# S4D layer and gated FFN on Trainium2: the stage-1 order taken from a table of ranks, with first table steps on POOL and norms that may run on DVE

## The chip, the cores and the metric

One core of a Trainium2 chip. The engines that matter are PE (TensorE: matmul; PEld is its weight load), DVE (VectorE), ACT (ScalarE), POOL (GpSimd) and SP (SyncE, which issues the DMAs). Each runs its own instructions in the order in which the program gives them, and waits on semaphores where it needs another engine's result. The metric is device time of one execution, in us; lower is better.

## The reference

One transformer-like layer on a sequence of L = 2048 rows of D = 640 numbers: a modulated LayerNorm, a state-space convolution (S4D, N = 128 states per channel), a residual, a second modulated LayerNorm and a gated FFN of width F = 1728.

```python
mod = (_silu(c) @ w_mod).reshape(c.shape[0], 6, 1, -1)
sa, ca, ga, sb, cb, gb = (mod[:, 0], mod[:, 1], mod[:, 2], mod[:, 3], mod[:, 4], mod[:, 5])
h = _layernorm(x) * (1 + ca) + sa
x = x + ga * A(h)
h = _layernorm(x) * (1 + cb) + sb
x = x + gb * B(h)

def A(u):
    dt = jnp.exp(log_dt)
    A = -jnp.exp(log_A_real) + 1j * A_imag
    C = (C_real + 1j * C_imag) * dt[:, None]
    P = jnp.exp((A * dt[:, None])[:, :, None] * pos[None, None, :])
    K = 2.0 * jnp.einsum("dn,dnl->dl", C, P).real
    y = irfft(rfft(u, 2 * L) * rfft(K, 2 * L), 2 * L)[:L]
    return y + u * D_skip

def B(x):
    return (silu(x @ w1) * (x @ w3)) @ w2
```

## The kernel before

**Stage 1** makes K, the convolution and the residual; **stage 2** is the FFN. Stage 1 works on five blocks of 128 channels. A block has eight chunks of 16 channels, and each half of a block (four chunks) has a table of angles in integers.

- *Tables* (`tables`, tasks `t<block>.<half>.<i>`): `begin` makes five shifted copies of the step (tiles `p`, `step`, from `pS`), `first` a copy of `pB`, and four additions on POOL fill the table.
- *Chunks* (`gen_tasks`, tasks `g<block>.<chunk>.`): `ph` on POOL adds two tables to 1024 angles per partition; `z0` to `z2` on POOL make the sizes (tiles `yy`, `xx`); `s0` to `s4` on ACT are the sines (`tr`, in PSUM); `m0` to `m4` on DVE multiply sizes and sines; `p` on PE sums over the states (`kps`); `r` and `d` copy the result to `ks`.
- *First LayerNorm*: `mean`, `sq` and `hscale` make the statistics (`xs`, `h_st`, `h_mv`, `h_nm`); in `h_tasks`, `l` loads x, `n` (function `h_norm`) normalises into PSUM (`hn`), `x` and `a` on DVE apply the modulation, and `hb` is stored and read again as `xb`.
- *Spectra*: tasks `hh` and `k` are the first transforms of `xb` and `ks` on PE (`ps`), copied to `sp`. Tasks `w<block>.<i>` (`spectrum_tasks`) hold for each of eight groups `f` (`fh`, copied to `hz`), `k` (`fk`), the products `x0`, `x1`, `c` on DVE (`fp`), and for each pair of groups the first inverse transform `z` (`fz`), copied to `zt` (tasks `v0`, `v1`) and stored as `zd`.
- *Ahead of stage 2*: `iz0`, `iz1` read `zd` back, `ir0`, `ir1` (`first_rows`) do the last inverse transform of the first rows (`iy`) on PE with the residual `x` and the LayerNorm statistics `st_n` on DVE; `fw` and `fs` load and split the first FFN weights (`wl`, `w2l`).

The parameters come from `param_tasks`: chain `pa` for all blocks, then `pb` and `pc` for block 0 (k = 0) and for blocks 1 to 4 (k = 1), each step a task, and `turn_steps` (`q<k>.`: transposes `ptp` on PE, copies to `pB`, `pS`, `mag`).

**What sets the order.** Everything of stage 1 is added as a task to a `Plan` (line 101): the engines that it may run on with a duration for each, what it comes after, a rank, and the ring slots that it takes and gives back (for instance two `ph`, two `yy`, two `xx`, three `tr`, four PSUM banks `bank`). `place` (line 119) is a list scheduler with these durations: of the tasks that could start soonest on an engine, the lowest rank goes next, and a task with two engines goes to the one that it would leave first. `run` calls it with ranks that are written by hand; then four times (`ROUNDS`) `back` runs the plan from its end, and `place` takes the late times that result as ranks. The instructions are then written out in that order. On the chip no plan exists: each engine has its order, and semaphores do the rest.

**Stage 2** does the FFN in four blocks of 512 rows, with hidden columns in 14 pieces; its first matmul is `gu` (line 753), and its order doesn't come from the plan.

Of the kernel before, what the change touches and what calls it, by code (L numbers as in the profile page):

```python
# [32 lines left out]
ROUNDS = 4  # L33
# [67 lines left out]
class Plan:  # L101
# [99 lines left out]
    def back(self, rank, order):  # L201

        T = self.tasks
        index = {n: i for i, n in enumerate(T)}
        before, left = {n: list(t[3]) for n, t in T.items()}, dict.fromkeys(T, 0)
        users, taken = {}, {r: [] for r in self.n}
        for n, t in T.items():
            for k in t[7]:
                users.setdefault(k, []).append(n)
        for _, _, _, n in order:  # L210
            for r, x, _ in T[n][6]:
                if len(taken[r]) >= self.n[r]:
                    before[n] += users[r, taken[r][len(taken[r]) - self.n[r]]]
                taken[r].append(x)
        later = {n: [] for n in T}
        for n, x in before.items():
            for a in x:
                later[a].append(n)
                left[a] += 1
        late = {n: len(x) for n, x in later.items()}  # L220
        end, at, free, port, line, table = {}, {}, dict.fromkeys(self.LAG, 0.0), 0.0, 0.0, None
        ready = [n for n in T if not late[n]]
        while ready:
            best = {}
            for n in ready:
                engs, took, _, _, _, shared, _, _, _, dma = T[n]
                c = None
                for j, e in enumerate(engs):
                    s = 0.0
                    for a in later[n]:  # L230
                        s = max(s, end[a] + (self.LAG.get(e, 0.0) if at[a] != e else self.CHAIN.get(e, 0.0)))
                    if e and not dma:
                        s = max(s, free[e])
                    if e and shared and e != "ACT":
                        s = max(s, port)
                    if c is None or s + took[j] < c[0]:
                        c = s + took[j], s, e, j
                best.setdefault(c[2], []).append((c[1], rank[n], index[n], n, c[2], took[c[3]]))
            pick = None
            for c in best.values():  # L240
                m = min(x[0] for x in c) + self.NEAR
                x = min((y for y in c if y[0] <= m), key=lambda y: y[1:3])
                if pick is None or x[:3] < pick[:3]:
                    pick = x
            s, _, _, n, e, took = pick
            ready.remove(n)
            _, _, _, _, _, shared, _, _, tab, dma = T[n]
            if tab and e == "ACT":
                took, table = took + (self.TABLE if table and tab != table else 0.0), tab
            fin = s + took  # L250
            if dma:
                for b in dma:
                    line = max(s, line) + b / self.RATE
                fin = line + self.LAND + self.FLY
            elif e:
                free[e] = fin
                if shared and e != "ACT":
                    port = fin
            end[n], at[n] = fin, e
            for m in before[n]:  # L260
                late[m] -= 1
                if not late[m]:
                    ready.append(m)
        return end
# [12 lines left out]

class K:
# [248 lines left out]
    def tables(self, b, h):  # L527
# [25 lines left out]
        return [(("DVE", "POOL"), (.75, 2.2), begin),  # L553
# [477 lines left out]
    def gen_tasks(self, b):  # L1031
# [33 lines left out]
        for c in range(8):  # L1065
# [7 lines left out]
            for i in range(5):  # L1073
                add(n + f"s{i}", "ACT", 1.02 if i == 2 else .55, lambda c=c, i=i: ch[c][2](i), [n + f"s{i - 1}" if i else n + "ph"], t + 1 + .1 * i,
                    table=None if i == 2 else "sin", take=[] if i == 2 else [("tr", 1)], give=[("ph", n + "ph")] if i == 4 else [])
# [6 lines left out]
            add(n + "r", "ACT", .3, lambda c=c: rows(c), [n + "p"] + ([f"k{b - 1}.{i}.m" for i in range(8)] if b else ["exp0", "q0.t0", "q1.t0"]), t + 3, give=[("kg", n + "p")])  # L1082
            add(n + "d", "DVE", .1, lambda c=c: skip(c), [n + "r"] + (["dsk"] if b == 0 else []), t + 3, give=[("kg", n + "p")])

    def h_tasks(self, b):
        V, A, G = self.nc.vector, self.nc.scalar, self.nc.gpsimd
        add, W = self.plan.add, self.W
        for i in range(4):
# [7 lines left out]
            add(n + "n", "ACT", 1.54, lambda i=i, place=place: self.h_norm(b, i, place()), [n + "l", "hscale"], t, take=[(bank, 1)],  # L1096
# [7 lines left out]
    def first_tasks(self, b, m):  # L1104
# [23 lines left out]
        for i in range(8):  # L1128
# [14 lines left out]
    def spectra_tasks(self, b):  # L1143
# [56 lines left out]
        for i in range(8):  # L1200
# [50 lines left out]
    def param_tasks(self, T, prio):  # L1251
# [35 lines left out]
    def early_tasks(self, e):
# [136 lines left out]
    def weights_of(self):  # L1424
# [38 lines left out]
```

## Time and profile before

| | us |
|---|---|
| median of 3 runs | 1041.65 |
| lowest and highest run | 1037.33, 1042.3 |
| the profiled execution | 1041.82 |
| its span, first to last instruction | 1039.7 |
| PE busy in the span | 896.2 (86%) |
| DVE busy | 657.7 (63%) |
| ACT busy | 522.5 (50%) |
| POOL busy | 271.1 (26%) |
| mean granted clock of PE | 0.947 |

The shares are means over two stages that have little in common: POOL is nearly idle in stage 2, and PE is nearly always busy there. Stage 1 ends at 436.5 us with the first `gu`. A line of the trace gives the start and the duration of an instruction, and in brackets how long its engine had been idle and what ended that. All instructions that a task issues carry the line of the helper that records them (L90 before, L156 with the change), so groups are told apart by tile and shape.

### The profile page before, as it was taken

The page shows a single profiled execution, that of the slowest core. Times are in us where ns is not written, and L with a number is a line of the kernel's source. Part 1 is how long each engine was busy: PE and PEld are TensorE (multiplying, and loading weights), DVE is VectorE, ACT ScalarE, POOL GpSimd, SP SyncE. Part 2 cuts the span into 40 slices and gives each one's busy share as a digit, 9 for nine tenths or more (in the row PEclk, how much of TensorE's full clock was granted, in tenths as well). Part 3 has the DMA queues.
Part 4 walks back from the last instruction along what each step waited for, and adds up shares of the span by engine and source line. Part 5 has one row for each costly group of instructions (what it writes and reads, how often), then busy time and mean ns, then how long its engine had stood idle before and what let it go on. Part 6 is the DMA issues. An engine that isn't in the chain of part 4 may idle for free.

```text
span 1039.7 us, 20267 instructions
## 1 busy us (share of the span) xinstructions
PE 896.2 (86%) x8129; PEld 715.9 (69%) x8129; DVE 657.7 (63%) x1200; ACT 522.5 (50%) x876; POOL 271.1 (26%) x268
## 2 busy tenths in 40 slices
PE   1454676879899986599999999999999999999996
PEld 1123555667688773477788888888888888888884
DVE  6988888898999945467675353464454454544332
ACT  5659798998778851233234252343343333433221
POOL 1785878877888500000000000000000000000000
PEclk9877888999999997599999999999999999999999
DMA  9872443442222393987432354332453333542402
GB/s 197 268 261 59 123 123 85 119 106 63 63 81 46 97 258 114 212 201 169 118 114 77 99 131 113 94 86 74 114 153 88 104 87 89 140 114 76 113 14 51
DMA packets 140998, 122.05 MB, mean 117 GB/s; under 512 B 13416, under 2 KB 124776, under 8 KB 139368
## 3 DMA queue, kind: packets, MB, share of 16 engines
q1 hardware_dynamic: 140904, 120.75, 43.8%
q8 instruction: 64, 1.05, 0.4%
q14 instruction: 30, 0.25, 0.1%
HBM read 99.75 MB, written 20.97 MB: 116 GB/s over the span
## 4 chain that ended last, share of the span: by engine, by line
PE 59%; DVE 1%; DMA 1%; ACT 0%; SPq 0%; issue 0%; ACTq 0%; DVEq 0%
PE gu L753 12%; PE gu L754 12%; PE gu L755 12%; PE acc L788 6%; PE acc L789 6%; PE acc L790 6%; PE iy L647 2%; PE fz L90 1%; PE tp L680 1%; PE to L804 1%; PE fk L90 1%; PE acc L793 0%; PE acc L794 0%; DMA izb<-zd 0%; PE iy L90 0%; PE fh L90 0%
## 5 line engine op out<-in xcount | busy, mean ns | idle before, releaser
L754 PE MATMUL gu<-xl,wh 128*128 128x512 f32 x540 | 212.9, 394 | 0.0
L753 PE MATMUL gu<-xh,wh 128*128 128x512 f32 x540 | 212.5, 394 | 0.5 <-ACT xh L683 0.5
L755 PE MATMUL gu<-xh,wl 128*128 128x512 f32 x540 | 211.9, 392 | 0.0
L658 ACT ACTIVATE wh<-wr 128x640 fp32r<-128x640 f32 x105 | 71.9, 731 | 136.0 <-PE gu L754 134.8
L721 POOL MEMSET w2l<- 64x640 f32 x3 | 1.9, 628 | 451.9 <-PE acc L789 451.9
L753 PEld LDWEIGHTS gu<-xh,wh 128*128 128x128 f32 x540 | 102.1, 189 | 25.6 <-issue 1.0
L754 PEld LDWEIGHTS gu<-xl,wh 128*128 128x128 f32 x540 | 102.0, 189 | 21.9
L755 PEld LDWEIGHTS gu<-xh,wl 128*128 128x128 f32 x540 | 102.0, 189 | 21.9
L788 PE MATMUL acc<-ah,w2h 128*128 128x512 f32 x260 | 103.8, 399 | 0.0
L789 PE MATMUL acc<-ah,w2l 128*128 128x512 f32 x260 | 102.2, 393 | 0.0
L767 ACT ACTIVATE th<-gu 128x512 f32<-128x512 f32 x52 | 31.1, 599 | 136.6 <-PE gu L755 136.6
L768 DVE SCALAR_TENSOR_TENSOR a<-th,gu 128x512 f32<-128x512 f32 x52 | 35.8, 688 | 100.4 <-ACT th L767 100.2
L769 DVE TENSOR_TENSOR a<-a,gu 128x512 f32<-128x512 f32 x52 | 35.8, 688 | 97.0 <-PE gu L755 97.0
L790 PE MATMUL acc<-al,w2h 128*128 128x512 f32 x260 | 96.4, 391 | 0.0
L90 POOL TENSOR_TENSOR yy<-e,e 128x512 f32<-128x512 f32 x80 | 85.0, 1082 | 29.5 <-PE kps L90 25.4
L659 DVE TENSOR_TENSOR wl<-wr,wh 128x640 fp32r<-128x640 f32 x105 | 82.2, 819 | 10.6 <-ACT wh L658 10.6
L90 POOL TENSOR_TENSOR ph<-p,p 128x1024 int32<-128x1024 int32 x40 | 78.3, 1962 | 27.6 <-ACT tr L90 24.6
L90 PE MATMUL kps<-yy,xx 128*32 128x64 f32 x2560 | 53.9, 244 | 33.2 <-DVE xx L90 28.7
L90 PEld LDWEIGHTS kps<-yy,xx 128*32 128x32 f32 x2560 | 47.5, 123 | 47.9 <-issue 40.1
L658 ACT ACTIVATE w2h<-w2r 128x640 fp32r<-128x640 f32 x51 | 37.6, 738 | 81.5 <-issue 42.5
L90 DVE TENSOR_TENSOR yy<-yy,tr 128x512 f32<-128x512 f32 (+1 forms) x80 | 75.6, 945 | 4.6 <-ACT tr L90 4.2
L659 DVE TENSOR_TENSOR w2l<-w2r,w2h 128x640 fp32r<-128x640 f32 x51 | 42.0, 823 | 56.3 <-ACT w2h L658 56.0
(202 smaller groups left out, 1650.5 us busy)
## 6 DMA issues: line engine op xcount, KB each, us to landing
wr<-in_w SPq DMA_DIRECT2D x104, 320.0 KB, 3.9
w2r<-in_w SPq DMA_DIRECT2D x52, 320.0 KB, 3.0
zd<-zt SPq DMA_DIRECT2D x40, 256.0 KB, 2.4
iz<-zd SPq DMA_DIRECT2D x24, 320.0 KB, 6.3
xs<-in_x SPq DMA_DIRECT2D x16, 320.0 KB, 12.2
hs<-hb SPq DMA_DIRECT2D x20, 256.0 KB, 2.5
xb<-hs SPq DMA_DIRECT2D x20, 256.0 KB, 4.8
x<-in_x SPq DMA_DIRECT2D x16, 320.0 KB, 8.7
```

What stands on the lines that cost most here:

```text
L90: self.prev = self.k.order(f(*a, **kw), self.prev)
L658: self.nc.scalar.activation(H, v, AF.Copy)
L659: eng.tensor_tensor(Lo, v, H.bitcast(F32), op=ALU.subtract)
L753: nc.tensor.matmul(pg, wh[:, i, k, :], xh[:, k, :], start=(k == 0), stop=False)
L754: nc.tensor.matmul(pg, wh[:, i, k, :], xl[:, k, :], start=False, stop=False)
L755: nc.tensor.matmul(pg, wl[:, i, k, :], xh[:, k, :], start=False, stop=(k == KT - 1))
L767: nc.scalar.activation(th, gu[0], AF.Tanh, scale=0.5)
L768: nc.vector.scalar_tensor_tensor(a, th, 1.0, gu[0], op0=ALU.add, op1=ALU.mult)
L769: nc.vector.tensor_mul(a, a, gu[1])
L788: nc.tensor.matmul(acc[k], w2h[:, sl], ah, start=(m == 0), stop=False)
L789: nc.tensor.matmul(acc[k], w2l[:, sl], ah, start=False, stop=False)
L790: nc.tensor.matmul(acc[k], w2h[:, sl], al, start=False, stop=(m == 12))
```

## The change

Six things change; what is computed stays the same.

1. A table `RANKS` holds one integer for each task, in the order in which the tasks are added; `place` runs once with it. `back` and the rounds go.
2. `begin` of the first table (block 0, first half) is tied to DVE, the other nine to POOL. Before, the scheduler chose.
3. `h_norm` may run on ACT or on DVE, where it is a `tensor_scalar`. Before, it was tied to ACT.
4. The ten last parameter steps of block 0 (`pc0`) are one task on DVE.
5. Block 1's first statistics move from DVE to ACT (`stat_v`).
6. Some durations that the scheduler reckons with are set to those of a trace, and a table step also waits for `q.v0`.

```diff
-ROUNDS = 4
+RANKS = """
+-1152 -1540 -1534 -1515 -1509 -1417 -1345 -1436 -1412 -1402 -1385 -1330 -1273 -1351 -1452 -1478 -1480 -1475 -1459 -1510 -1507
...
+"""
...
-    def run(self, rounds):
+    def run(self):
 
         T = self.tasks
-        self.order = self.place({n: t[4] for n, t in T.items()})
-        for i in range(rounds):
-            late = self.back({x[3]: -x[1] for x in self.order}, self.order)
-            self.order = self.place({n: -x for n, x in late.items()})
+        found = [int(x) for x in RANKS.split()]
+        assert not found or len(found) == len(T)
+        self.order = self.place(dict(zip(T, found)) if found else {n: t[4] for n, t in T.items()})
...
-        return [(("DVE", "POOL"), (.75, 2.2), begin),
+        return [("DVE", .9, lambda: begin("DVE")) if b == h == 0 else ("POOL", 1.9, lambda: begin("POOL")),
...
-    def h_norm(self, pc, b, out):
+    def h_norm(self, pc, b, out, e):
...
-            self.nc.scalar.activation(out[:, j], x[:, j], AF.Identity, scale=rstd[:, s], bias=nb[:, s])
+            if e == "DVE":
+                self.nc.vector.tensor_scalar(out[:, j], x[:, j], rstd[:, s], nb[:, s], op0=ALU.mult, op1=ALU.add)
+            else:
+                self.nc.scalar.activation(out[:, j], x[:, j], AF.Identity, scale=rstd[:, s], bias=nb[:, s])
...
-                add(n + f"s{i}", "ACT", 1.02 if i == 2 else .55, ...
+                add(n + f"s{i}", "ACT", (.52, .52, .95, .62, .62)[i], ...
...
-            add(n + "n", "ACT", 1.54, lambda i=i, place=place: self.h_norm(b, i, place()), [n + "l", "hscale"], t, take=[(bank, 1)],
+            add(n + "n", ("ACT", "DVE"), (1.95, .85), lambda e, i=i, place=place: self.h_norm(b, i, place(), e), [n + "l", "hscale"], t, take=[(bank, 1)],
...
-            c = chain(f"pc{k}.", end, n, {0: [b]}, prio + .3 + k * later)
+            if k:
+                c = chain(f"pc{k}.", end, n, {0: [b]}, prio + .3 + k * later)
+            else:
+
+                c = "pc0"
+                add(c, "DVE", 3.1, lambda end=end: [f(self.nc.vector) for _, f in end], [b], prio + .3, port=True)
...
-                add(f"stp{b_}", None, 0, None, [q + "v2"])
+                add(f"stp{b_}", None, 0, None, [q + "v0", q + "v2"])
...
-        add("hscale", "DVE", 5.0, scale, ...
+        add("hscale", "DVE", 6.5, scale, ...
...
-            stat=lambda b: 15.0 + 6 * b, stat_v=(1, 3), later=5.0, col=50.0, quick=20.0, late=3.0, tail=S(4))
+            stat=lambda b: 15.0 + 6 * b, stat_v=(3,), later=5.0, col=50.0, quick=20.0, late=3.0, tail=S(4))
```

Durations of `r`, `e`, `h`, `c`, `v` and `fold` in the plan change by a few per cent as well.

How often an instruction stands in the program, before and after: table copies `step<-pS` on DVE 15 and 3, `p<-pS` on DVE 10 and 2, the five POOL operations of `begin` 25 and 45; `hn` on ACT 80 and 28, on DVE 0 and 52; statistics `h_st` on DVE 16 and 8, `xs` sums and `xs` squares on ACT 8 and 12 each; `zt` on DVE 12 and 7, on ACT 28 and 33; sine and exponent table loads on ACT 14 and 12.

The order of the instructions moves at many places. Three of them follow. First DVE at the start, where the last parameter steps of block 0 (tiles `wb`, `xb`, `e11` at 128x128; those at 128x512 belong to blocks 1 to 4) lead to block 0's `pB`. Before:

```order
L90 TENSOR_TENSOR xb_86<-xb_86 128x512
L90 TENSOR_TENSOR e11_120<-e11_120 128x128
L90 TENSOR_TENSOR xb_86<-e21_121 128x512
L90 SCALAR_TENSOR_TENSOR wb_84<-e11_120,wb_84 128x128
L90 SCALAR_TENSOR_TENSOR wb_84<-xb_86,wb_84 128x512
L90 SCALAR_TENSOR_TENSOR xb_86<-e11_120,xb_86 128x128
L90 SCALAR_TENSOR_TENSOR wb_84<-xb_86,wb_84 128x512
L90 SCALAR_TENSOR_TENSOR xb_86<-xb_86,dt_133 128x128
L90 TENSOR_TENSOR e11_120<-e11_120 128x512
L90 TENSOR_SCALAR pB_124<-ptp0_229 128x128
L90 COPY mag_127<-ptp0_229 128x128
```

With the change:

```order
L156 TENSOR_TENSOR xb_86<-e21_121 128x128
L156 SCALAR_TENSOR_TENSOR wb_84<-xb_86,wb_84 128x128 x2
L156 TENSOR_TENSOR e11_120<-e11_120 128x128
L156 SCALAR_TENSOR_TENSOR wb_84<-e11_120,wb_84 128x128
L156 SCALAR_TENSOR_TENSOR xb_86<-e11_120,xb_86 128x128
L156 SCALAR_TENSOR_TENSOR xb_86<-xb_86,dt_133 128x128
L156 TENSOR_SCALAR pB_124<-ptp_243 128x4x128
L156 TENSOR_SCALAR e11_120<-pB_124 128x512
L156 TENSOR_SCALAR pS_125<-pB_124 128x4x128
L156 COPY mag_127<-ptp0_229 128x128
L156 TENSOR_SCALAR pB_124<-ptp0_229 128x128
```

The operations of the other blocks that stood between block 0's steps are behind them now, and the other blocks' `pB`, `e11` and `pS` are in front of block 0's `pB`.

Second, PE from the last product of the last chunk (`kps` with `yy_624`) on, where `ps40i` are first transforms of `xb`, `ps41i` those of `ks` and `fh4i`, `fk4i` the spectra. Before:

```order
L90 MATMUL kps_387<-yy_624_4546,xx_624_4545 32x64 x32
L90 MATMUL ps407_4781<-wk_72,xb_86 64x4x16x2 x8
L90 MATMUL ps410_4814<-wk_72,ks4_4158 64x4x16x2 x8
L90 MATMUL ps411_4829<-wk_72,ks4_4158 64x4x16x2 x8
L90 MATMUL ps412_4839<-wk_72,ks4_4158 64x4x16x2 x8
L90 MATMUL ps413_4849<-wk_72,ks4_4158 64x4x16x2 x8
L90 MATMUL ps414_4865<-wk_72,ks4_4158 64x4x16x2 x8
L90 MATMUL ps415_4875<-wk_72,ks4_4158 64x4x16x2 x8
L90 MATMUL ps416_4885<-wk_72,ks4_4158 64x4x16x2 x8
L90 MATMUL ps417_4895<-wk_72,ks4_4158 64x4x16x2 x8
L90 MATMUL fh40_4905<-sp_85,wb_84 64x128 x8
```

With the change:

```order
L156 MATMUL ps413_4770<-wk_72,ks4_4117 64x4x16x2 x8
L156 MATMUL ps414_4781<-wk_72,ks4_4117 64x4x16x2 x8
L156 MATMUL kps_378<-yy_624_4565,xx_624_4564 32x64 x32
L156 MATMUL ps411_4824<-wk_72,ks4_4117 64x4x16x2 x8
L156 MATMUL ps415_4857<-wk_72,ks4_4117 64x4x16x2 x8
L156 MATMUL ps417_4872<-wk_72,ks4_4117 64x4x16x2 x8
L156 MATMUL ps416_4882<-wk_72,ks4_4117 64x4x16x2 x8
L156 MATMUL fh40_4892<-sp_85,wb_84 64x128 x8
L156 MATMUL fk40_4908<-sp_85,wb_84 64x128 x8
```

Four first transforms stand behind the last product where nine stood. Further on, the two groups of `iy` (of `ir0`) were ahead of the second `fz`, and are ahead of the last pair of spectra now. Before:

```order
L90 MATMUL fh45_5063<-sp_85,wb_84 64x128 x8
L90 MATMUL iy0_0_5079<-iz00_4951,wd_4805 64x512
L90 MATMUL iy0_0_5079<-iz01_4952,wd_4805 64x512
L90 MATMUL iy1_0_5083<-iz00_4951,wd_4805 64x512
L90 MATMUL iy1_0_5083<-iz01_4952,wd_4805 64x512
L90 MATMUL fz410_5099<-fp42_4990,wz_73 128x512
L90 MATMUL fz411_5100<-fp42_4990,wz_73 128x512
L90 MATMUL fz410_5099<-fp42_4990,wz_73 128x512
L90 MATMUL fz411_5100<-fp42_4990,wz_73 128x512
L90 MATMUL fk45_5105<-sp_85,wb_84 64x128 x8
```

With the change:

```order
L156 MATMUL fh45_5033<-sp_85,wb_84 64x128 x8
L156 MATMUL fz410_5044<-fp42_4985,wz_73 128x512
L156 MATMUL fz411_5045<-fp42_4985,wz_73 128x512
L156 MATMUL fz410_5044<-fp42_4985,wz_73 128x512
L156 MATMUL fz411_5045<-fp42_4985,wz_73 128x512
L156 MATMUL fk45_5070<-sp_85,wb_84 64x128 x8
L156 MATMUL fh46_5094<-sp_85,wb_84 64x128 x8
L156 MATMUL fk46_5103<-sp_85,wb_84 64x128 x8
L156 MATMUL iy0_0_5119<-iz00_4990,wd_4848 64x512
L156 MATMUL iy0_0_5119<-iz01_4991,wd_4848 64x512
L156 MATMUL iy1_0_5123<-iz00_4990,wd_4848 64x512
```

Third, DVE in front of the last inverse transform, which needs `fp46` complete. Before:

```order
L90 TENSOR_TENSOR fp46_5153<-fk46_5131,hz46_5140 128x2x2x128
L90 TENSOR_TENSOR fk46_5131<-fk46_5131,hz46_5140 128x512
L90 TENSOR_TENSOR fp46_5153<-fp46_5153,fk46_5131 128x256 x2
L90 COPY zt421_5177<-fz421_5156 128x512
L90 TENSOR_TENSOR x20_4806<-iy2_0_5181,x20_4806 128x512
L90 TENSOR_TENSOR x20_4806<-iy3_0_5185,x20_4806 128x512
L90 BN_STATS st_n0_4812<-x20_4806 128x6 x8
L90 TENSOR_TENSOR fp46_5153<-fk47_5166,hz47_5162 128x2x2x128
L90 TENSOR_TENSOR fk47_5166<-fk47_5166,hz47_5162 128x512
L90 TENSOR_TENSOR fp46_5153<-fp46_5153,fk47_5166 128x256 x2
```

With the change:

```order
L156 TENSOR_TENSOR fp44_5042<-fp44_5042,fk45_5070 128x256 x2
L156 TENSOR_TENSOR fp46_5115<-fp46_5115,fk46_5103 128x256 x2
L156 TENSOR_TENSOR fp46_5115<-fk47_5151,hz47_5160 128x2x2x128
L156 TENSOR_TENSOR fk47_5151<-fk47_5151,hz47_5160 128x512
L156 TENSOR_TENSOR fp46_5115<-fp46_5115,fk47_5151 128x256 x2
L156 COPY zt420_5174<-fz420_5162 128x512
L156 TENSOR_TENSOR x20_4849<-iy2_0_5184,x20_4849 128x512
L156 TENSOR_TENSOR x20_4849<-iy3_0_5188,x20_4849 128x512
L156 BN_STATS st_n0_4855<-x20_4849 128x6 x8
```

The sums and the statistics of `iy2`, `iy3` stood ahead of the last three steps of `fp46`, and stand behind all of them now. The splits `wl0`, `w2l0`, which stood in front of the products `fp42`, are in front of those of `fp44`.

More of the change, by code (lines that the diff above doesn't have):

```diff
@@ L199, in place @@
         return order
-    def back(self, rank, order):
+    def run(self):
         T = self.tasks
[L204 to L264, printed above, removed]
@@ L1073, in gen_tasks @@
             for i in range(5):
[L1074 removed]
+                add(n + f"s{i}", "ACT", (.52, .52, .95, .62, .62)[i], lambda c=c, i=i: ch[c][2](i), [n + f"s{i - 1}" if i else n + "ph"], t + 1 + .1 * i,
                     table=None if i == 2 else "sin", take=[] if i == 2 else [("tr", 1)], give=[("ph", n + "ph")] if i == 4 else [])
@@ L1136, in first_tasks @@
             add(n + "m", "PE", 1.04, lambda i=i: mm(i), after + old, t, take=[(bank, 1)])
-            add(n + "e", ("ACT", "DVE"), (.49, .61), lambda e, i=i: out(i, e), [n + "m"], t - W["quick"], give=[(bank, n + "m")])
+            add(n + "e", ("ACT", "DVE"), (.48, .61), lambda e, i=i: out(i, e), [n + "m"], t - W["quick"], give=[(bank, n + "m")])
     def spectrum(self, b, m):
@@ L1209, in spectra_tasks @@
             add(n + "f", "PE", 1.0, lambda i=i: of(0, i), first + room, t, take=[("bank", 1)])
-            add(n + "h", "ACT", .49, lambda i=i: hold(i), [n + "f"], t - q, take=[("hz", 1)], give=[("bank", n + "f")])
+            add(n + "h", "ACT", .48, lambda i=i: hold(i), [n + "f"], t - q, take=[("hz", 1)], give=[("bank", n + "f")])
             add(n + "k", "PE", 1.0, lambda i=i: of(1, i), firstk + room + [n + "f"], t + .1, take=[("bank", 1)])
@@ L1213, in spectra_tasks @@
             add(n + "x1", "DVE", .61, lambda i=i: product(i, 1), [n + "x0"], t - q, give=[("hz", n + "h")])
-            add(n + "c", "DVE", .8, lambda i=i: both(i), [n + "x1"], t - q, give=[("bank", n + "k")])
+            add(n + "c", "DVE", .67, lambda i=i: both(i), [n + "x1"], t - q, give=[("bank", n + "k")])
             if i % 2 == 0:
@@ L1221, in spectra_tasks @@
             for f in range(2):
-                add(n + f"v{f}", ("ACT", "DVE"), (.49, .61), lambda e, j=j, f=f: out(j, f, e), [n + "z"], t - q, take=[("zt", 1)], give=[("bank", n + "z" + "'" * f)])
+                add(n + f"v{f}", ("ACT", "DVE"), (.48, .61), lambda e, j=j, f=f: out(j, f, e), [n + "z"], t - q, take=[("zt", 1)], give=[("bank", n + "z" + "'" * f)])
                 add(n + f"o{f}", "SP", 0, lambda j=j, f=f: store(j, f), [n + f"v{f}"], t, dma=[262144], give=[("zt", n + f"v{f}")])
@@ L1404, in fold @@
             V.tensor_mul(self.rB, self.rB, self.rows[2])
-        add("fold", "DVE", 1.5, fold, [f"rw{g}" for g in range(4)], 22, port=True)
+        add("fold", "DVE", 1.6, fold, [f"rw{g}" for g in range(4)], 22, port=True)
         add("wb", "SP", 0, lambda: nc.sync.dma_start(self.wb, self.t_wb), ["fold", "mr4", "lat1", "turn1"], 60, dma=[2097152])
```

7 lines of the change are left out of this document (3 added, 4 removed), and 64 rows, old and new, of the table RANKS.

## The prediction

> **What bounds the kernel now.** I read the profile's table of windows first, with cuts where the program changes character: the last multiply (m4) of each block's last chunk ends at 110.1, 181.0, 243.2, 313.5 and 361.5 us; 373.1 is the first spectrum matmul behind the last product, 414.0 the end of the loop of spectra, 436.5 the first FFN matmul. Columns are window, its us, busy us and instruction counts of PE, PEld, DVE, ACT and POOL, granted PE clock, DMA share, GB/s.
>
> ```profile
> 37.20:110.10 72.90, 35.17 (x636) 22.21 (x632) 63.20 (x118) 55.88 (x102) 56.33 (x46) 0.77 0.54 168
> 110.10:181.00 70.90, 47.15 (x917) 41.00 (x919) 59.91 (x105) 60.89 (x113) 57.51 (x58) 0.81 0.41 104
> 181.00:243.20 62.20, 50.98 (x993) 41.55 (x991) 56.09 (x96) 56.37 (x101) 52.56 (x52) 0.95 0.40 102
> 243.20:313.50 70.30, 64.00 (x1290) 52.77 (x1288) 64.58 (x114) 55.98 (x96) 56.47 (x55) 1.00 0.28 73
> 313.50:361.50 48.00, 46.17 (x1026) 38.60 (x1026) 45.56 (x81) 39.88 (x70) 34.50 (x28) 1.00 0.25 63
> 361.50:373.10 11.60, 10.73 (x231) 10.30 (x231) 0.33 (x2) 6.34 (x12) 0.63 (x1) 1.00 1.03 265
> 373.10:414.00 40.90, 30.58 (x310) 19.47 (x305) 26.57 (x59) 11.81 (x21) 0.00 (x0) 0.88 0.64 169
> 414.00:436.50 22.50, 8.25 (x37) 6.71 (x37) 9.24 (x32) 4.01 (x5) 1.27 (x1) 0.50 0.85 201
> 436.50:1039.70 603.20, 593.89 (x2676) 479.51 (x2676) 302.90 (x522) 210.97 (x323) 3.16 (x4) 0.99 0.40 106
> ```
>
> Three regimes. The FFN (603.2 us) has PE busy 593.9: nothing of this change is in it, and I carry it unchanged. Between 37.2 and 361.5 us four engines share the load: summed over the five blocks, DVE is busy 289.3 of 324.3 us (89%), ACT 269.0, POOL 257.4, and in the last block PE 46.17 of 48.00. So DVE is tightest, with 35 us idle. From 361.5 to 414.0 POOL has nothing, and PE and DVE pass the work to and fro. I call 361.5 T0: the sum is the shift of T0 plus the shift of the tail behind it. The waits of DVE and of POOL between 37.2 and 361.5 (total us, times, longest) are:
>
> ```profile
> DVE yy L90 <- ACT tr L90: 8.0, 6, 2.4
> DVE xx L90 <- ACT tr L90: 5.3, 5, 1.9
> DVE hn L90 <- ACT hn L90: 5.0, 8, 2.1
> ...
> POOL yy L90 <- PE kps L90: 25.4, 12, 6.4
> POOL ph L90 <- ACT tr L90: 24.6, 16, 4.8
> ```
>
> DVE's idle time is led by 18.3 us behind ACT's sines and norms; POOL idles because rings are given back late by ACT and PE.
>
> **The engines' loads.** The order of instructions gives exact counts before and after; the groups of instructions by shape (count, busy us, mean ns) give prices.
>
> ```profile
> L90 DVE TENSOR_SCALAR step<-pS 128x128 int32<-128x128 int32 x15 | 9.6, 691 | 0.0
> L90 DVE TENSOR_SCALAR p<-pS 128x128 int32<-128x128 int32 x10 | 4.8, 484 | 0.0
> L90 POOL TENSOR_TENSOR step<-p 128x128 int32<-128x128 int32 x10 | 4.3, 426 | 0.8
> L90 POOL COPY p<-pS 128x128 int32<-128x128 int32 x5 | 2.1, 421 | 0.1
> L90 ACT ACTIVATE hn<-xq,rs_n_h,rs_y_h 128x128 f32<-128x128 f32 x64 | 29.5, 461 | 5.5 <-DVE hb L90 3.9
> L90 DVE TENSOR_SCALAR pS<-ptp 128x128 int32<-128x128 f32 x1 | 0.3, 284 | 0.0
> L90 DVE COPY rsw<-rs_w_h 128x16 f32<-128x16 f32 x3 | 0.5, 178 | 0.1
> L90 DVE BATCH_NORM_STATS2 h_st<-xs 128x6 f32<-128x320 f32 x16 | 6.6, 476 | 1.0 <-DMA xs<-in_x 1.0
> L90 DVE COPY zt<-fz 128x512 f32<-128x512 f32 x12 | 8.1, 684 | 5.3 <-issue 3.6 <-PE fz L90 1.6
> L90 DVE TENSOR_TENSOR xx<-tr,xx 128x512 f32<-128x512 f32 x80 | 54.5, 683 | 5.7 <-ACT tr L90 5.3 <-POOL xx L90 0.3
> ```
>
> First table steps: four move from DVE to POOL. DVE loses 4 x (3 x 0.691 + 2 x 0.484) = 12.2 us; POOL gains 4 x 5 x about 0.42 = 8.4. Norms: 52 of 80 instructions (13 of 20 tasks) move from ACT to DVE. ACT loses 52 x 0.461 = 23.9. DVE's norm from SBUF into PSUM isn't in the trace: the lower end is 0.178 (a copy from SBUF into PSUM, an eighth of the columns: 9.3 us in all), the upper 0.691 (the table step of its size: 35.9). I take 0.284, the same operation and size with its other side in PSUM: 14.8 us, near the low end. Block 1's statistics leave DVE: 8 x 0.476 = 3.8, and ACT gains some 7.7 for their squares and sums. Five outputs zt go from DVE (5 x 0.684 = 3.4) to ACT (3.0), and two sine-table loads of ACT go (2.6). The other small moves come to about -0.3 for DVE and +0.7 for POOL. In sum **DVE -4.8, ACT -15.8, POOL +9.1 us**; the steps of pc0 are the same ten instructions in one piece, and PE's and SP's counts stay.
>
> On the tightest engine that is -4.8 (bounds by the norm: -10.3 and +16.3). POOL's +9.1 I charge at nothing, because its waits above hold 50 us in which the work can lie; without that cover it costs its 9.1. The norms also bring a wait to an end: 13 of 20 no longer come from ACT, so of the 5.0 us that DVE waited for hn 3.3 go. ACT, 15.8 us lighter, should be earlier with its sines: of the 13.3 us behind tr I take about a third, 4.7, since the other waits can be taken over by POOL's later phases. Together **-8** (bounds 0 and -18.3). A norm now queued on DVE waits for its load xq and a bank; the multiplies behind it, and through them the product on PE, would wait with it.
>
> **Port.** Here the trace must decide whether DVE is held up by POOL:
>
> ```profile
> 75.40 1.25 POOL L90 TENSOR_TENSOR pB<-pB,e 128x512 int32<-128x512 int32 x1
> 75.50 0.18 DVE L90 COPY rsw<-rs_w_h 128x16 f32<-128x16 f32 x1
> ...
> 117.20 1.96 POOL L90 TENSOR_TENSOR ph<-p,p 128x1024 int32<-128x1024 int32 x1
> 117.25 2.50 DVE L90 TENSOR_SCALAR step<-pS 128x128 int32<-128x128 int32 x2
> ```
>
> The table steps, SBUF to SBUF, wait: two took 2.50 us beside a phase. The copy into PSUM didn't: 0.18 us inside a POOL instruction of 1.25. The norm writes to PSUM like the copy, so I price it without a wait; that it waits is the rival D below. The Trainium skill ("SBUF — State Buffer", Who interferes with whom) has DVE and GpSimd share one port pair under an exclusive lock that a DVE instruction in a 2-port mode takes; and "VectorE: DVE Perf Modes" (Why PSUM operands drop a tier) excludes such a mode with a PSUM operand. By that D would not occur, and the 0.178 row agrees, though on 16 columns.
>
> **Start.** The first phase waits for block 0's pB. Its last parameter steps (128x128) alternate on DVE with wider ones of blocks 1 to 4, of which the first is shown:
>
> ```profile
> 25.86 0.68 DVE L90 TENSOR_TENSOR xb<-xb,wb 128x512 f32<-128x512 f32 x1
> 32.43 0.46 POOL L90 TENSOR_TENSOR pB<-pB,e 128x128 int32<-128x128 int32 x1 [4.97 <-DVE pB L90]
> 37.24 2.28 POOL L90 TENSOR_TENSOR ph<-p,p 128x1024 int32<-128x1024 int32 x1
> ```
>
> Eight such operations, some 5.3 us, stand ahead of block 0's pB; in the new order its ten steps are one piece, with about 2.2 us of other blocks' work around them. I take the first phase at about 34 instead of 37.24: **-3.0** (0 to -5).
>
> **Tail.** PE behind the last product, and DVE in front of the last inverse:
>
> ```profile
> 364.02 1.28 PE L90 MATMUL ps<-wk,xb 128*64 128x128 f32 x16
> 365.11 3.44 PE L90 MATMUL ps<-wk,ks 128*64 128x128 f32 x59
> 369.41 3.98 PE L90 MATMUL ps<-wk,ks 128*64 128x128 f32 x69 [0.87 <-issue]
> ...
> 379.68 1.99 PE L90 MATMUL fz<-fp,wz 64*128 64x512 f32 x8
> 393.23 3.17 PE L90 MATMUL fz<-fp,wz 64*128 64x512 f32 x8 [2.76 <-DVE fp L90]
> 400.60 1.99 PE L90 MATMUL fz<-fp,wz 64*128 64x512 f32 x8
> 404.58 1.52 DVE L90 TENSOR_TENSOR x<-iy,x 128x512 f32<-128x512 f32 x2 [1.23 <-PE iy L90]
> 406.02 1.63 DVE L90 BATCH_NORM_STATS2 st_n<-x 128x6 f32<-128x128 f32 x8
> 409.36 3.78 PE L90 MATMUL fz<-fp,wz 64*128 64x512 f32 x8 [3.99 <-DVE fp L90]
> ```
>
> Nine groups of first transforms stand there (16 + 59 + 69 = 144 matmuls), at about 1.03 us each; in the new order four, the others ahead of the last product: **-5.3**. They don't vanish: in a last block where PE is 96% busy I charge 4.5 groups, **+4.6**, to T0 (0 if PE finds its place).
>
> The loop of spectra: before, fz41 begins 393.23 - 379.68 = 13.6 us behind fz40, because iy0 and iy1 stand ahead of it on PE, and their sums, statistics and the four weight splits in front of its product on DVE. Without them it follows the product of fk43, about 6.8 us behind fz40: -6.8. Splits and sums now stand in front of fz42's product: +4.2 back. For fz43 the stretch from 400.60 to 409.36 loses the sums and statistics (1.52 + 1.63 and the 1.23 wait ahead of them) and overlaps with fz42: -6. I take **-9** for the loop's 40.9 us; the last outputs, both on ACT, +0.6.
>
> **Sum.** T0: -3.0 - 4.8 - 8 + 4.6 = -11.2. Tail: -5.3 - 9 + 0.6 = -13.7. The profiled execution took 1041.82 (its span is 1039.7), the median of the runs is 1041.65, so nothing is to be corrected: 1041.8 - 24.9 = **1017 us**.
>
> **The rivals.** A is the forecast, with its own range of 1006 to 1030: 0.52.
>
> B, POOL becomes the bound: with +9.1 it is the fullest engine in block 2, and DVE and ACT merely wait for its phases. Then T0 moves by -3.0 + 9.1, and 1041.8 + 6.1 - 13.7 = 1034. For it speaks that POOL has the long operations; against, that 24.6 us of its idle time come from ACT, which gets lighter. 0.13.
>
> C, the search's order removes all waits of DVE for ACT, and PE finds places for the groups: -3.0 - 4.8 - 18.3 - 13.7 gives 1002. Against: two engines at 83% can't both never be late. 0.14.
>
> D, slower: DVE's norms wait for POOL's running instruction as the table steps do. At the 1.25 us each of 117.25 a norm costs 0.97 more than I take, 52 of them 50 us: 1017 + 50 = 1067; at the mean of 0.691 it is +21: 1038. It makes the kernel slower by 0.5% from 0.58 us extra each (30 / 52). The copy's 0.178 speaks against it. 0.12, of which 0.08 above 1047.
>
> E, the moved table steps hold up DVE: the 8.4 us come back as DVE stalls, 1025. Against: xx takes 683 ns over 80 instructions beside a POOL that is 79% busy, no more than the copy zt with 684. 0.09. The Trainium skill ("Perfetto Trace Analysis", Optimizing Scalar/DVE Operations) warns in this sense that moving work between GpSimd and DVE may not help because they share the port. By that warning E's 1025 would stand; the 683 here doesn't bear it out.
>
> **How the numbers follow.** The range is 1000 to 1037: it holds A, B, C and E, and leaves out D's upper part and the far ends of the bounds. 0.5% is about what a measurement of this kernel can tell from no change. Faster: A, C, E and most of B, 0.82; within 0.5%: a rest of B and the lower part of D, 0.10; slower: D's upper part, 0.08.
>
> **What would show it.** Right: T0 near 350, first phase near 34, DVE norms near 0.28 us, their wait for ACT under 2 us, four groups behind the last product, the loop near 31 us, and an FFN of 603. POOL busy above 95% in some block speaks for B; norms above 0.6 us for D. An order whose ring waits turn up elsewhere makes the prediction wrong.

## The result and the profile after

The changed kernel takes 1013.06 us (median of 4 runs, 1010.92 to 1013.45) where before took 1041.68 on the same chip; the ratio is 0.973, with a 95% interval of 0.970 to 0.976. It is faster by 2.7%. The prediction was 1017 with a range of 1000 to 1037. The profiled execution took 1012.95 (its span is 1010.6), 28.9 us less than the one before, where 24.9 were forecast. Times and ratios below are of fast runs: one run of z2 (4871.78 us) and one of the kernel before in that series (3066.28) are left out as slow.

The table of windows of the changed kernel, cut at the same events as before (first phase, last multiply of each block, first spectrum, end of the loop, first `gu`; columns as before):

```profile
35.30:106.30 71.00, 39.67 (x656) 22.51 (x656) 64.40 (x114) 54.80 (x102) 64.49 (x59) 0.78 0.66 199
106.30:172.90 66.60, 52.75 (x1004) 42.93 (x1006) 63.25 (x122) 54.41 (x94) 57.35 (x60) 0.92 0.39 102
172.90:236.90 64.00, 53.42 (x1118) 45.41 (x1116) 62.53 (x118) 56.02 (x95) 56.64 (x57) 1.00 0.42 111
236.90:290.80 53.90, 49.42 (x1066) 42.58 (x1064) 51.86 (x96) 45.63 (x78) 49.16 (x50) 1.00 0.27 66
290.80:340.70 49.90, 49.31 (x1050) 41.76 (x1047) 48.51 (x88) 42.62 (x75) 39.44 (x34) 1.00 0.34 84
340.70:355.00 14.30, 9.91 (x223) 9.32 (x213) 0.33 (x2) 4.22 (x8) 0.63 (x1) 0.76 1.05 268
355.00:385.50 30.50, 27.78 (x304) 20.32 (x302) 23.45 (x49) 11.08 (x19) 0.00 (x0) 0.94 0.67 172
385.50:408.30 22.80, 9.65 (x45) 6.93 (x41) 12.19 (x42) 4.80 (x7) 1.27 (x1) 0.62 0.86 203
408.30:1010.60 602.30, 593.01 (x2676) 478.80 (x2676) 303.00 (x522) 210.81 (x323) 3.16 (x4) 0.99 0.40 107
```

T0, the last multiply, moved from 361.5 to 340.7: **-20.8 us**. From T0 to the first `gu` it was 75.0 us and is 67.6: **-7.4**. The FFN takes 0.9 less. Of the -20.8, 1.9 are the earlier first phase; blocks 0 and 1 are 1.9 and 4.3 us shorter, blocks 2 and 4 1.8 and 1.9 longer, and block 3 is 16.4 shorter (70.3 to 53.9): PE's work there fell from 64.0 to 49.4 us and DVE's from 64.6 to 51.9, because part of it now runs earlier, most of it in blocks 1 and 2 (PE's instructions: 224 fewer in block 3, 87 and 125 more in blocks 1 and 2). DVE's work up to T0 is what it was, 290.6 us against 289.3, but its idle time between first phase and T0 fell from 35.0 to 14.8 us (305.4 - 290.6).

The waits of DVE in that stretch (total us, times, longest) and the groups on which the sum rested:

```profile
DVE ks L156 <- PE kps L156: 3.1, 3, 1.4
DVE sp L156 <- PE ps L156: 2.9, 2, 2.5
DVE yy L156 <- POOL yy L156: 1.9, 2, 1.0
DVE ks L156 <- ACT hn L156: 1.0, 1, 1.0
DVE xx L156 <- ACT tr L156: 1.0, 2, 0.7
...
DVE yy L156 <- ACT tr L156: 0.6, 2, 0.4
```

```profile
L156 DVE TENSOR_SCALAR hn<-xq,rs_y_h,rs_n_h 128x128 f32<-128x128 f32 x44 | 18.2, 413 | 1.2
L156 DVE TENSOR_TENSOR hn<-hn,rw 128x512 f32<-128x512 f32 x20 | 13.9, 694 | 0.5 <-ACT hn L156 0.5
L156 DVE TENSOR_SCALAR step<-pS 128x128 int32<-128x128 int32 x3 | 0.7, 274 | 0.0
L156 DVE TENSOR_TENSOR xx<-tr,xx 128x512 f32<-128x512 f32 x80 | 54.6, 683 | 1.0 <-ACT tr L156 1.0
```

The waits for ACT that led the list before are nearly gone: behind sines 13.3 us then and 1.6 now, for norms 5.0 then and 0.5 now (the idle time of the second group here). A norm on DVE takes 413 ns, not the 284 that I took, and all four of a task 1.76 us, as in this row of the timeline:

```profile
110.86 1.76 DVE L156 TENSOR_SCALAR hn<-xq,rs_y_h,rs_n_h 128x128 f32<-128x128 f32 x4
```

The timeline of PE behind T0 shows where the tail didn't do what was forecast:

```profile
340.45 1.17 PE L156 MATMUL kps<-yy,xx 128*32 128x64 f32 x64
341.55 1.97 PE L156 MATMUL ps<-wk,ks 128*64 128x128 f32 x32
343.45 1.14 PE L156 MATMUL kps<-yy,xx 128*32 128x64 f32 x60
348.98 0.64 PE L156 MATMUL kps<-yy,xx 128*32 128x64 f32 x4 [4.39 <-issue]
349.54 5.64 PE L156 MATMUL ps<-wk,ks 128*64 128x128 f32 x64
355.02 1.09 PE L156 MATMUL fh<-sp,wb 128*64 128x128 f32 x16
```

The last product stops 4.39 us after 60 of its 64 matmuls, with no engine to wait for ("issue"), and the four groups behind it take 5.64 us, 1.41 each. Before, the longest such stop between first phase and `gu` is 2.20 us, and it stands elsewhere:

```profile
268.67 6.66 PE L90 MATMUL ps<-wk,ks 128*64 128x128 f32 x117 [2.20 <-issue]
```

### The profile page after: what moved, and what is told of

The parts are those of the page before. It is cut to its first block, busy times and chain, and to the rows that moved or that the text cites. A ratio compares the mean times of both kernels' runs of the same rounds, so it can differ in the third digit from the quotient of the medians.

```text
span 1010.6 us, 20260 instructions
## 1 busy us (share of the span) xinstructions
PE 891.2 (88%) x8129; PEld 714.0 (71%) x8129; DVE 656.8 (65%) x1214; ACT 507.8 (50%) x843; POOL 279.4 (28%) x288
## 3 DMA queue, kind: packets, MB, share of 16 engines
q8 instruction: 64, 1.05, 0.4%
## 4 chain that ended last, share of the span: by engine, by line
PE 73%; DVE 12%; DMA 6%; ACT 3%; issue 3%; SPq 1%; POOL 0%; DVEq 0%; ACTq 0%; POOLq 0%
PE gu L753 12%; PE gu L754 12%; PE gu L755 12%; PE acc L788 6%; PE acc L789 6%; PE acc L790 6%; PE ps L156 4%; DVE yy L156 3%; PE fk L156 3%; PE kps L156 2%; PE fh L156 2%; DMA sp<-in_w_mod 2%; PE fz L156 2%; DVE fp L156 2%; PE iy L647 2%
## 5 line engine op out<-in xcount | busy, mean ns | idle before, releaser
L156 POOL TENSOR_TENSOR yy<-e,e 128x512 f32<-128x512 f32 x80 | 86.3, 1095 | 16.6 <-PE kps L156 11.7
L156 PE MATMUL kps<-yy,xx 128*32 128x64 f32 x2560 | 51.3, 234 | 31.3 <-DVE xx L156 23.4
L156 PEld LDWEIGHTS kps<-yy,xx 128*32 128x32 f32 x2560 | 44.7, 116 | 41.2 <-issue 25.0
```

The source lines that it names most:

```text
L156: self.prev = self.k.order(f(*a, **kw), self.prev)
```

## The experiments

### Is it the order, or which engine does what?

All four of these keep one of the two orders of tasks as it is and change only the engine on which some tasks are written out: the line in `run` that emits a task takes the engine from a small table.

```diff
-                T[n][2](e)
+                T[n][2](at.get(n, e))
```

The other edits (`pc0` in one piece, block 1's statistics on ACT, the engines of `zt`) stay with their order: y1 to y3 have them, y4 doesn't.

**y1**: the changed kernel, `at` puts the 13 norms that run on DVE back on ACT.

> The changed kernel with its order of tasks, but all 20 norms on ACT. Theory O (the order of the table removed the waits): DVE loses 13 x 4 x 0.413 = 21.5 us of work, ACT gains 24 and is then busy about 277 of 305 us up to the last multiply; DVE's new waits for hn and the work taken away about cancel, 1011 to 1019 us. Theory A (the waits went because ACT was relieved of the norms): the waits of DVE for hn and sines return, 13 to 18 us in all, and the time is 1021 to 1031 us.

Measured: 1027.77 us, ratio to before 0.988 (0.986 to 0.990). That is in theory A's range. T0 is at 356.1, 15.4 later than with the change. **y2**: the changed kernel, `at` puts four first table steps back on DVE.

> The changed kernel with its order of tasks, but four of the nine first table steps that it has on POOL back on DVE (blocks 0.1, 1.0, 1.1, 4.0, as before). DVE gains some 12 us of work (its steps beside POOL take 0.69 us), POOL loses 8.4. Theory D (DVE is the tightest engine up to the last multiply, 290 of 305 us busy in the changed kernel): 5 to 12 us slower than the changed kernel, 1018 to 1025. Theory P (POOL's phases set the pace as well): the two cancel, 1011 to 1015 us.

Measured: 1016.61 us, 0.977 (0.976 to 0.979), between the two ranges and nearer D's; T0 at 344.6 is 3.9 later. DVE has 4.3 us more to do (294.88 in y2), not 12, since its table steps cost less there than before, when some of them ran beside a phase (the group in y2; 691 ns before):

```profile
L156 DVE TENSOR_SCALAR step<-pS 128x128 int32<-128x128 int32 x15 | 3.4, 274 | 0.0
```

**y3**: both together, so the new order with the engines of before.

> The changed kernel's order of tasks with the engines of before: norms on ACT, those four table steps on DVE. Theory O: most of the gain stays, 1013 to 1023 us. Theory A (the other engines are the gain): only the tail's share of 7 us and the start's 2 are left of it, 1030 to 1036 us.

Measured: 1030.9 us, 0.992 (0.990 to 0.993): theory A again. T0 is at 360.6, within a microsecond of before. **y4**: the order of before; 13 norms on DVE and the four table steps on POOL.

> The kernel before with its own order of tasks, but 13 norms on DVE and those four table steps on POOL, as in the change. Theory O: no gain, 1037 to 1047 us, since the waits that the order makes stay. Theory A: the first stage's gain of 15 to 20 us appears, 1021 to 1027 us.

Measured: 1046.02 us, 1.005 (1.003 to 1.007): theory O's range, not A's, and T0 at 367.0 is 5.5 later than before. y1 and y3 spoke for A, so neither theory holds for all: the order alone moves T0 by one microsecond, the engines alone make it worse, and the two together take 20.8 us off. The views of windows from first phase to T0 say why (y1, y3 and y4, each a view of its own kernel):

```profile
35.10:356.10 321.00, 252.50 (x4879) 202.31 (x4873) 272.32 (x479) 274.55 (x490) 267.23 (x257) 0.91 0.41 111
```

```profile
35.00:360.60 325.60, 249.26 (x4877) 200.51 (x4881) 276.70 (x499) 274.60 (x490) 258.82 (x237) 0.90 0.41 110
```

```profile
36.20:367.00 330.80, 250.07 (x4848) 199.81 (x4846) 295.67 (x543) 248.88 (x426) 265.74 (x255) 0.87 0.38 103
```

DVE's idle time is the window less its busy time: 48.7 us in y1, 48.9 in y3, 35.1 in y4, against 35.0 before and 14.8 with the change. In y4 ACT has 20 us less to do than before (248.9 against 269.0), and DVE's idle time stays: its waits for sines and norms do fall, from 18.3 to 11.2 us, but others come in their place, above all for POOL's sizes (6.3 us, 0.3 before). The rows of y4, to which 1.2 us for norms are to be added:

```profile
DVE yy L90 <- ACT tr L90: 6.3, 5, 3.2
DVE yy L90 <- POOL yy L90: 6.3, 7, 2.7
DVE xx L90 <- ACT tr L90: 3.7, 4, 1.4
```

So T0 moves with DVE's work: +6.3 us of work and a first phase 1.0 earlier make +5.5. In y1 and y3 DVE has 14 to 18 us less to do than with the change, but waits 34 us more. What for, shows the view of waits of y1:

```profile
DVE hn L156 <- ACT hn L156: 17.3, 9, 5.2
DVE xx L156 <- ACT tr L156: 6.0, 6, 2.0
DVE ks L156 <- ACT ks L156: 4.9, 3, 3.0
DVE yy L156 <- ACT tr L156: 3.0, 4, 2.0
```

In the new order DVE comes to the modulation right behind a norm. On DVE the norm ahead of it costs 1.76 us in its own queue; on ACT it costs up to 5.2 us of waiting, and DVE waits for sines longer too (9.0 us, 1.6 with the change).

**v1** asks whether the changed tasks and durations need the table at all: all edits except the merging of `pc0`, but the four rounds of before in place of `RANKS`. (Its list scheduler put 15 norms on DVE.)

> The changed kernel's tasks and durations (all edits but the merging of pc0), ranked as before, by hand and four rounds, in place of the table; 15 of the 20 norms then run on DVE. Theory S (the gain needs an order that was searched for these engines; each half alone gains nothing before the last multiply): 1036 to 1048 us. Theory T (tasks and durations as traced are enough for any ranking): 1013 to 1025 us.

Measured: 1038.38 us, 0.998 (0.996 to 1.000): theory S. From first phase to T0 its windows read:

```profile
32.50:367.20 334.70, 258.56 (x4889) 203.47 (x4890) 307.58 (x550) 248.76 (x429) 266.79 (x257) 0.88 0.39 109
```

DVE has 17.0 us more to do than with the table (307.6 against 290.6) and idles 27.1. ACT is at 248.8, as light as in y4, and DVE idles 7.9 us less than before; but it has 18.3 us more to do than before, and T0, at 367.2, is later.

### The loop of spectra

**y5**: the kernel before, four tasks moved in the order that is written out.

```diff
+        for n, m in [("fs0", "w4.3.c"), ("fs1", "w4.4.c"), ("ir0", "w4.6.h"), ("ir1", "z4.3.v1")]:
+            x = self.order.pop([y[3] for y in self.order].index(n))
+            self.order.insert([y[3] for y in self.order].index(m) + 1, x)
```

> The kernel before with only four tasks of the loop of spectra moved: the weight splits behind fp42's products, iy0 and iy1 behind fk46, iy2 and iy3 with their statistics behind the last inverse transform and its copies. If the loop's order is the cause, the loop goes from 40.0 us to about 31 and the time to 1031 to 1034 us; if the loop waits for transfers (DMA share 0.64 there), it stays within 2 us of before, 1039 to 1042.

Measured: 1034.0 us, 0.992 (0.991 to 0.994), inside the first range for the time. The loop on PE, from its first spectrum to its last `fz`:

```profile
373.02 1.13 PE L90 MATMUL fh<-sp,wb 128*64 128x128 f32 x16
...
386.88 1.99 PE L90 MATMUL fz<-fp,wz 64*128 64x512 f32 x8 [1.57 <-DVE fp L90]
...
397.57 3.86 PE L90 MATMUL fz<-fp,wz 64*128 64x512 f32 x8 [1.85 <-DVE fp L90]
...
404.53 3.53 PE L90 MATMUL fz<-fp,wz 64*128 64x512 f32 x8 [2.02 <-DVE fp L90]
```

The loop takes 35.0 us (373.02 to 404.53 + 3.53) instead of 40.0, not the 31 expected; the change's takes 30.0 (355.02 to the end of its last `fz` at 385.0). So the places of four tasks give half of the loop's gain. That the rest comes from the finer order of products and spectra is not shown, since that order wasn't tried by itself. The same transfers are done in 5.0 us less, so these 5.0 us weren't due to them. That the time came into its range although the loop missed its own was luck: the first `gu` is 6.4 us earlier, and the rest of the 8 us lies in the FFN, which the edit doesn't touch.

### PE's gap behind T0

In every kernel with the new order and the old place of the loads the gap stands at the same place, behind 59 or 60 of the last product's 64 matmuls, 4.39 to 4.72 us long (y1, y2, y3, y6 and z2 too); before, the one behind T0 is 0.87 us and in a first transform. **y7**: the changed kernel, the loads of the first FFN weights (`fw0`, `fw1`) written out behind the second spectrum.

> The changed kernel with the loads of the first FFN weights (1.3 MB) issued some 15 us later, behind the second spectrum. If PE's gap of 4.4 us inside the last product comes from its own instructions arriving late behind the burst of loads (DMA share 1.05 there), the gap shrinks to under 1.5 us and the first spectrum comes within 11 us of the last multiply instead of 14.3; the time falls by 1 to 4 us if the weight splits don't become late in return, else it rises by up to 4. If the burst is not its cause, the gap stays at 4 to 5 us.

Measured: 1011.22 us, 0.971 (0.969 to 0.972), and the gap stays at 4.63 us. The weights alone are not its cause, and the time isn't clearly less than the change's own, since the intervals overlap. **z1**: `x`, `wd`, the weights and `iz0` all behind the first stored output.

```diff
+        for n, m in [("change", "z4.0.o0"), ("fx", "change"), ("fw0", "fx"), ("iz0", "fw0"), ("fw1", "iz0")]:
```

> The changed kernel with the whole burst of loads (x, wd, the first weights, 3.9 MB) issued behind the first stored output of the loop of spectra instead of at the last multiply. If PE's gap of 4.4 to 4.7 us in the last product comes from the burst, it goes (under 1 us), and the first spectrum comes 4 us earlier after the last multiply; the last inverse of the first rows and the splits then wait for their loads, so the time as a whole may rise by up to 15 us. If the gap comes from the place in PE's instruction stream alone, it stays at 4.4 to 4.7.

Measured: 1021.56 us (one run). The gap is gone, the last product runs in one piece, and the first spectrum comes 7.4 us behind the last multiply (347.96 - 340.56, where the multiply starts at 339.88 and takes 0.68) instead of 14.3. The loads are then late: PE waits 12.63 us in the loop. **w1** tries to have both: one transfer of 512 bytes that reads block 4's last kernel values, ahead of the burst.

```diff
             self.x2 = [self.xp.tile([P, 4, D], F32, name="x20")]
+            nc.sync.dma_start(self.pace, self.ks[4][:, 31, 63:64])
             self.load_x2(0)
```

> The changed kernel with one more small transfer (512 bytes of block 4's kernel values to memory) ahead of the burst of loads, so that the burst waits for the last product instead of starting 6 us before its end. If the burst keeps PE's instructions from arriving, the last product runs without its gap (under 1 us instead of 4.4), the first spectrum comes some 8 us after the last multiply instead of 14.3, and 4 to 6 us are saved if no later instructions are held up in turn: 1006 to 1009 us. If the gap merely moves to the next piece of PE's instructions, or the splits wait for their weights, 1011 to 1015 us.

Measured: 1015.47 us, 0.976 (0.973 to 0.980): half a microsecond above the second case, no gain over the change. The timeline of w1 has the product without its gap and the loop behind it:

```profile
341.75 1.38 PE L156 MATMUL kps<-yy,xx 128*32 128x64 f32 x64
343.07 3.71 PE L156 MATMUL ps<-wk,ks 128*64 128x128 f32 x64
346.61 1.08 PE L156 MATMUL fh<-sp,wb 128*64 128x128 f32 x16
...
367.99 1.98 PE L156 MATMUL fh<-sp,wb 128*64 128x128 f32 x16 [3.62 <-ACT zt L156]
```

and the first split of a weight, on ACT and then on DVE, late by its load:

```profile
364.62 0.74 ACT L156 ACTIVATE wh<-wr 128x640 fp32r<-128x640 f32 x1 [4.53 <-DMA wr<-in_w]
...
365.38 0.83 DVE L156 TENSOR_TENSOR wl<-wr,wh 128x640 fp32r<-128x640 f32 x1 [5.31 <-ACT wh L156]
```

The first spectrum comes 7.6 us behind the last multiply (346.61 - 339.0), as expected, and the loop grows from 30.0 to 39 us, because splits and inverse wait for what was loaded some 7 us later. **w2**: w1 with the weights also behind the second spectrum.

> The same with the first FFN weights also issued behind the second spectrum (as in y7), which halves the burst and lets the loads of the inverse go first. If loads of weights were what delays in the paced kernel, 1 to 3 us less than w1; if the weight splits become late, 1 to 4 us more.

Measured: 1014.96 us, 0.976 (0.973 to 0.979), the same as w1. The burst causes the gap; moving it costs what the gap costs, and no version here clearly beats the change.

The view of DMA queues shows what comes late. It names one queue "instruction" (q8: 64 packets, 1.05 MB in the whole program, so some 16 KB each); in the last block of the changed kernel it brings a packet every 4 to 7 us. In z1, w1 and w2 one packet starts 0.7 to 0.9 us behind T0. In the seven kernels with the gap this packet starts 5.7 to 6.1 us behind T0, the loads' queue takes a DMA share of 0.97 to 1.00 up to then, and PE goes on 1.3 to 1.6 us after the packet's end; the packet ahead of it came 8.1 to 8.5 us before T0 in all ten. The row in the changed kernel (window 346.3 to 349.0; from 332.5 to 346.3 there is none, and the packet starts at 346.5):

```profile
q8 instruction: 1, 0.02, 2.5%
```

and in w1 (window 339.0 to 341.5; it starts at 339.9):

```profile
q8 instruction: 1, 0.02, 3.4%
```

The rows don't say whose instructions these are; that they are PE's is inferred from PE going on behind them.

### What a norm on DVE costs

**y6**: the changed kernel, where a norm on DVE multiplies by 20 and adds 0 instead of using the row's statistics, so this part of the LayerNorm is left out.

```diff
-                self.nc.vector.tensor_scalar(out[:, j], x[:, j], rstd[:, s], nb[:, s], op0=ALU.mult, op1=ALU.add)
+                self.nc.vector.tensor_scalar(out[:, j], x[:, j], 20.0, 0.0, op0=ALU.mult, op1=ALU.add)
```

> The changed kernel with the norms on DVE taking two constants instead of two per-partition scalars (the statistics are left out of these norms, so the output changes). If the 0.413 us of a norm come from reading its two scalars, it takes 0.28 us here, as the copy pS<-ptp of the same size does; if they come from writing to PSUM, it stays at 0.41. The time falls by at most 52 x 0.13 = 7 us: 1006 to 1013 us.

Measured: 1006.17 us (one run). The group of norms on DVE in y6:

```profile
L156 DVE TENSOR_SCALAR hn<-xq 128x128 f32<-128x128 f32 x44 | 12.9, 293 | 1.8 <-ACT sp L156 0.6
```

With constants a norm takes 293 ns, so the two per-partition scalars cost 120 ns of the 413. T0 is at 335.8, 4.9 us earlier for 52 x 0.12 = 6.2 us less work on DVE. **z2**: the same norm as two operations on 128x512 with the scalars repeated along the columns.

```diff
+                if j == 0:
+                    q = slice(4 * b, 4 * b + 4)
+                    self.nc.vector.tensor_tensor(out, x, bc(rstd[:, q], 2, P), op=ALU.mult)
+                    self.nc.vector.tensor_tensor(out, out, bc(nb[:, q], 2, P), op=ALU.add)
```

> The changed kernel with each norm on DVE as two operations of 128x512 (times the scale, plus the shift, both repeated along the columns) instead of four of 128x128 with two scalars each. Four norms take 1.76 us now; two operations of the kind hn<-hn,rw start 0.6 us apart, so 1.2 to 1.3 us: 13 x 0.5 = 6.5 us less for DVE. If DVE's work before the last multiply counts one to one, 1006 to 1009 us; if its idle time takes it up, 1012 to 1014; if the operation with both inputs outside PSUM waits for POOL, up to 0.6 us more each and 1013 to 1018.

Measured: 1016.92 us, 0.978 (0.975 to 0.981), inside the third case. Its two groups:

```profile
L156 DVE TENSOR_TENSOR hn<-xq,rs_y_h 128x512 f32<-128x512 f32 x11 | 13.7, 1246 | 0.1
L156 DVE TENSOR_TENSOR hn<-hn,rs_n_h 128x512 f32<-128x512 f32 x13 | 9.1, 700 | 0.4
```

The second operation has one input in PSUM and takes 700 ns; the first reads both from SBUF and takes 1246, between 0.69 us (at 182.24, where POOL ran nothing as it began) and 2.48 (at 167.22, just behind the start of a phase). The Trainium skill ("SBUF — State Buffer", Who interferes with whom) says that a DVE instruction with two SBUF inputs contends with a GpSimd instruction that reads SBUF; these rows agree.

## Why the prediction was right, point by point

The time is 4 us under the forecast and in its range. By its own steps the sum came out of two errors that offset each other: T0 moved by -20.8 where -11.2 were forecast, and the stretch from T0 to the first `gu` by -7.4 where -13.7 were. That the total is so close is luck.

- **Start**: -3.0 forecast; the first phase came at 35.34 instead of 37.24, so -1.9, inside its bounds.
- **DVE's load**: -4.8 forecast (its terms add up to -4.9); it is +1.3 (290.6 against 289.3). The term that was mis-sized is the norm: 52 at 0.413 us are 21.5 us instead of the 14.8 that I charged. I took the price of an operation with constants; y6 measures 0.293 for just that.
- **Waits for ACT**: -8 forecast with a bound of -18.3; they fell by 16.2 us (18.3 to 2.1), and DVE's whole idle time by 20.2. This is the term that was too small. Its reason was also wrong in part: I let 8 us of them go because ACT loses 15.8 us of work, and only the rest be taken over by other waits. y4 has ACT lighter by 20 us: these waits fall by 7.1, and DVE's idle time is unchanged, because others take over all of it. v1 has ACT lighter by 20 us too, and T0 is later by 5.7. What removes the waits is norms on DVE in an order made for that: the same order with norms on ACT idles 48.7 us (y1).
- **PE's groups ahead of T0**: +4.6 charged. The last block grew by 1.9 (48.0 to 49.9), with PE busy 49.3 us of it. The charge didn't come: start, work and idle time of DVE (-1.9, +1.3, -20.2) already add up to the -20.8, and DVE's idle time outside the waits for ACT fell too, from 16.7 to 12.7 us. One reason that fits, though no run tests it by itself, is that earlier groups of PE had been spread out as well: block 3, where PE and DVE were both over 90% busy, lost 14.6 us of PE work, most of it to blocks 1 and 2. I had looked at the order of the last block alone.
- **Groups behind the last product**: -5.3 forecast; from T0 to the first spectrum it is +2.6 (11.7 to 14.3). w1, with the same order and no gap, takes 7.6: so the order itself gives -4.1, and 6.7 are the gap (4.4), the slower groups behind it (5.64 against w1's 3.71, 1.9) and 0.4 in the product itself. The gap is what failed here: of such stops in the trace of before my rows held the one of 0.87 us, and I gave it no term; the one of 2.20 us I didn't show. The remaining 1.2 are a miscount: two of the groups that stand ahead of the last product in the order still run behind T0 (341.55), since PE is busy with the product before them until then, so three groups were saved and not five; the 0.87 us that w1 doesn't have make up for part of that.
- **The loop**: -9 forecast, -10.0 measured (40.0 to 30.0 us). y5 shows that the places of the splits and of `iy` are a cause of it, for half. My working (whose terms add up to -8.6) gave these places nearly all of it, so here the number is better than its reason.
- **From the loop's end to the FFN, and the FFN**: 23.3 us as before, so the +0.6 for the last outputs doesn't show, and 602.3 against 603.2.

Of the rivals, C (all waits go, PE finds places) describes the stretch to T0 best, without its DVE term; my argument against it, two engines at 83%, was true of ACT alone, since POOL was at 79%. B didn't come: POOL is 87% busy up to T0 (the five windows: 267.1 of 305.4), and at most 91% in a block. D is refuted: none of the 52 norms takes more than 416 ns, whatever POOL does. E is refuted by y2: on DVE the moved steps cost 3.9 us of T0, so on POOL they don't come back as stalls, and `xx` still takes 683 ns.

One thing stays open: how much of the gain could be had with norms on ACT in an order searched for that. It wasn't tried.

## What to carry to other kernels

An assignment of work to engines and an order belong together: test each without the other before you credit one of them. Here the order alone was worth 0.9 us up to T0, the assignment alone less than nothing, and both together 20.8 us. Relieving an engine gains only where the order lets the others start earlier; read the idle time of the tightest engine, and ask which instruction in its queue will wait next. A group that is moved ahead of a waiting instruction counts as moved only if its engine has time for it before that wait ends.

## What the hardware showed unexpectedly

- A 128x128 `tensor_scalar` of DVE from SBUF into PSUM takes 293 ns with two constants and 413 with two per-partition scalars.
- PE stood still for 4.4 to 4.7 us beside a burst of loads (DMA share 1.05), always at the same place; with the burst elsewhere (z1, w1) that gap went, and w1 has one of 0.88 us at another place. A packet of the instruction queue came some 5 us later beside the burst than without it. The Trainium skill ("Runtime: NRT & Kernel Launch", Instruction fetch mechanics) has each engine fetch its program in 16 KiB blocks through a DMA queue of its own, at a cost that is mostly hidden. The 64 packets of 1.05 MB agree with such blocks; if the late one is PE's, its cost was not hidden here.
- After that gap PE ran slower. The windows of the four groups behind the product, in the changed kernel and in w1 (PE's clock is the third number from the end):

```profile
349.50:355.00 5.50, 5.50 (x66) 5.46 (x66) 0.17 (x1) 2.17 (x4) 0.63 (x1) 0.63 1.13 269
```

```profile
343.00:346.60 3.60, 3.60 (x67) 3.53 (x66) 0.17 (x1) 2.17 (x4) 0.63 (x1) 1.00 1.08 42
```

The granted clock is 0.63 behind the gap and 1.00 without it, for the same 64 matmuls. The Trainium skill ("TensorE: Matmul & The Clock Gate", Part 1: The HAM clock gate) says that the clock falls to half after an idle window of some 3.4 us. A gap of 4.4 us followed by a mean of 0.63 agrees.
